# A 64-byte read of every ninth row of the modulation weights ahead of the loads of a DiT block

## The chip, the cores and the metric

The kernel runs on one core of a Trainium2 chip. The metric is device time in microseconds (us) of one execution; the median of several executions is compared. The profiled execution is one such execution, recorded by the hardware profiler; its span runs from the first to the last instruction of the program.

## The reference, cut to what matters

The reference is one DiT block (a diffusion transformer layer) on B, N, D = 2, 256, 1152, with 2 heads of 576 and an MLP of 4608; all inputs are bf16. The six modulation vectors come from the small input `c` through the weights `w_mod`.

```python
mod = (_silu(c) @ w_mod).reshape(B, 6, 1, D)
shift_a, scale_a, gate_a, shift_m, scale_m, gate_m = [mod[:, i] for i in range(6)]
h = _layernorm(x, axis=-1) * (1 + scale_a) + shift_a
qkv = (h @ wqkv).reshape(B, N, 3, H, Dh)
...
attn = _softmax(jnp.einsum('bqhd,bkhd->bhqk', q, k) * Dh ** (-0.5), axis=-1)
a = jnp.einsum('bhqk,bkhd->bqhd', attn, v).reshape(B, N, D) @ wo
x = x + gate_a * a
h2 = _layernorm(x, axis=-1) * (1 + scale_m) + shift_m
m = _gelu(h2 @ w_fc1) @ w_fc2
return x + gate_m * m
```

`w_mod` is a matrix of 1152 rows and 6912 columns. A row has 13,824 bytes, the whole 15.9 MB. Columns D to 2D hold `scale_a`.

## The kernel before, in words

The 512 tokens lie in four tiles of 128 partitions. All weights are streamed from HBM once, through one ordered list of loads on SyncE's queue (`dma`, L665, with `eng="sp"`): `x` in two loads (`ld_x0`, `ld_x1`), the scale columns of `w_mod` (`ld_sc0_*`: three loads, the first 640 columns of `scale_a`, in runs of 1280 bytes), the K weights row block by row block (`ld_wk*`), the rest of the scale columns (`ld_sc5_*`, runs of 1024 bytes of the same rows), and then the shift columns, Q, V, the other modulation columns, the output projection and the MLP weights. Only one load goes elsewhere: `c` (18 pieces of 256 bytes, `ld_c`, L692) is issued on ScalarE's queue.

The kernel builds a list of units with dependencies, and a planner (`Sched.schedule`, L281) puts them in order by a simple model of durations and landing times. TensorE (PE) and SyncE keep the order in which the program writes them. The first steps of VectorE (DVE) and ScalarE (ACT) are a list by hand (`S.first`, L909 to L915); the rest follows the planner. Every unit then waits on semaphores for what it depends on. A unit that writes a region of SBUF waits for the earlier writers of that region.

The start of the program, which the prediction follows step by step, is this:

- GpSimd (POOL) makes the identity matrix (L708 to L711); PE does two filler matmuls `warm_a` of 512 columns (L716 to L718).
- PE transposes `c` (`c_T`, L721), ScalarE takes its tanh (`c_tanh`, L722), VectorE turns it into SiLU (`c_half`, `c_silu`, L723 and L724). On PE 15 more filler matmuls `warm_b` (L773, called in L820) follow.
- VectorE (tiles 1 and 2) and ScalarE (tiles 0 and 3) take the LayerNorm statistics of `x` (`ln_stats_dve` L728, `ln_stats_act` L737), GpSimd the power -0.5, and VectorE writes the normalised rows (`xn_1`, `xn_0`, L753).
- PE transposes them (`xn_T`, L760), and between them multiplies the scale columns with SiLU(c), 128x2 at a time (`mod_kt`, L775), with single fillers between these (`warm_c`, `warm_d`, `warm_e`).
- VectorE adds 1 (`sc1a`, L783), then VectorE and ScalarE scale the transposed rows (`hk`, L786 to L792), and PE starts the K projection (`k_pair`, L804).

After that come Q, the scores and softmax, V, the transposes of the probabilities (`pt_transposes`, L953, whose copies write the tiles `PTS` at the offset `O_PT`), attention, output projection with the second LayerNorm, and the two MLP products.

All matmuls go through the helper at L686 and all transposes through L689, so these two lines stand for all of PE's work in the profile; all DMAs have L667.

Of the kernel before, what the change touches and what calls it, by code (L numbers as in the profile page):

```python
# [497 lines left out]
P = 128  # L498
NTOK = 512
D = 1152  # L500
KT = 9
# [40 lines left out]
def build_kernel(nc, x, c, wqkv, wo, w_mod, w_fc1, w_fc2, out):  # L542
# [5 lines left out]
    with (  # L548
# [4 lines left out]
        def sb(off, nbytes, dt=BF16):  # L553
            assert off % 4 == 0 and off + nbytes <= ARENA_BYTES, (off, nbytes)
            v = arena[:, off // 2:(off + nbytes) // 2]
            if dt == F32:
                v = v.bitcast(F32)
            return v
# [18 lines left out]
        O_PT = O_P + 4096  # L577
# [87 lines left out]
        def dma(dst, src, nbytes, name, is_out=False, eng="sp", run=4096):  # L665
            eff = 1.0 if run >= 4096 else (1.08 if run >= 2304 else (1.15 if run >= 1536 else (1.3 if run >= 1024 else 1.42)))
            return S.op(eng, 500.0 if eng == "sp" else 150.0, lambda e: e.dma_start(dst, src), reads=[src], writes=[dst],  # L667
                        name=name, dma_bytes=nbytes * eff, is_out=is_out)
# [20 lines left out]
            S.instr(lambda e: e.transpose(o, i_, idn), reads=[i_, idn], writes=[o])  # L689


        dma(CSB[0:18, :], c.rearrange("b (k p) -> (b k) p", p=P), 18 * 256, "ld_c", eng="act")  # L692
        for b in range(2):
            dma(X[:, 2 * b:2 * b + 2, :], xv[b], 2 * P * D * 2, "ld_x%d" % b)
# [200 lines left out]
        for kt in range(KT):  # L895
            for b in range(2):
# [5 lines left out]
                else:  # L902
# [7 lines left out]
            "dve": ["zq4b", "c_half", "c_silu", "bn_ln1_1_0", "bn_ln1_1_1", "bn_ln1_1_2", "aggr_ln1_1", "veps_ln1_1", "bn_ln1_2_0", "nvar_ln1_0", "veps_ln1_0",  # L910
                    "xn_1", "xn_0", "bn_ln1_2_1", "bn_ln1_2_2", "aggr_ln1_2", "veps_ln1_2", "nvar_ln1_3", "veps_ln1_3",
                    "sc1a_0", "hk_0_0", "xn_2", "hk_1_0", "xn_3", "hk_3_0", "hk_0_1", "hk_1_1", "hk_3_1", "hk_4_1", "sc1a_5"],
            "act": ["ld_c", "c_tanh", "sq_ln1_0", "sum_ln1_0", "sq_ln1_3", "sum_ln1_3", "xnT_cp0_8", "xnT_cp0_5", "hk_2_0", "hk_4_0",
                    "hk_2_1", "xnT_cp1_8", "xnT_cp1_5"],
        }  # L915

# [285 lines left out]
def bass_standalone__dit_block__diffusion_kernel(  # L1202
    nc: bass.Bass,
    x: bass.AP,
    c: bass.AP,
    wqkv: bass.AP,
    wo: bass.AP,
    w_mod: bass.AP,
    w_fc1: bass.AP,
    w_fc2: bass.AP,  # L1210
    out: bass.AP,
):
    build_kernel(nc, x, c, wqkv, wo, w_mod, w_fc1, w_fc2, out)
# [28 lines left out]
```

## Time and profile before

| what | value |
|---|---|
| median of 3 runs | 246.3 us (246.1 to 247.2) |
| profiled execution | 246.26 us |
| its span | 244.2 us |
| PE busy | 239.3 us, 98% of the span |
| weight loads on PE (PEld) | 146.8 us, 60% |
| VectorE busy | 98.7 us, 40% |
| ScalarE busy | 63.0 us, 26% |
| GpSimd busy | 21.5 us, 9% |
| read from HBM | 50.14 MB |

Times in the profile count from the start of the span. In the timeline a line begins with the start and the duration, then come engine, line, operation and form; a number after `x` is how many instructions are merged, and square brackets give the idle time ahead of it and what ended it. A name with a q (ACTq, SPq) is the queue of an engine's sequencer: there a DMA is issued, while the data move later. In the list of DMA issues the last number is the median time from issue to landing. In the chain of work that ended last a line has start, duration, engine and line.

### The profile page before, as it was taken

The page shows a single profiled execution, that of the slowest core. Times are in us where ns is not written, and L with a number is a line of the kernel's source. Part 1 is how long each engine was busy: PE and PEld are TensorE (multiplying, and loading weights), DVE is VectorE, ACT ScalarE, POOL GpSimd, SP SyncE. Part 2 cuts the span into 40 slices and gives each one's busy share as a digit, 9 for nine tenths or more (in the row PEclk, how much of TensorE's full clock was granted, in tenths as well). Part 3 has the DMA queues.
Part 4 walks back from the last instruction along what each step waited for, and adds up shares of the span by engine and source line. Part 5 has one row for each costly group of instructions (what it writes and reads, how often), then busy time and mean ns, then how long its engine had stood idle before and what let it go on. Part 6 is the DMA issues. An engine that isn't in the chain of part 4 may idle for free.

```text
span 244.2 us, 3973 instructions
## 1 busy us (share of the span) xinstructions
PE 239.3 (98%) x1721; PEld 146.8 (60%) x1731; DVE 98.7 (40%) x205; ACT 63.0 (26%) x128; POOL 21.5 (9%) x37
## 2 busy tenths in 40 slices
PE   7999999999999999999999999999999999999995
PEld 2689844466557666798544444444565656566575
DVE  3742450446323689879999600000022222111112
ACT  5730340235312306983322333222000000000000
POOL 1400000000021275600000110000000000000000
DMA  6999999999994999979943589200000000000000
GB/s 244 350 377 393 389 381 401 419 422 406 387 329 111 341 386 391 392 246 396 349 132 101 172 256 393 79 0 3 0 16 16 19 17 16 19 16 16 29 22 16
DMA packets 28875, 51.57 MB, mean 211 GB/s; under 512 B 1587, under 2 KB 15675, under 8 KB 28859
## 3 DMA queue, kind: packets, MB, share of 16 engines
q1 hardware_dynamic: 28384, 50.14, 56.9%
q0 software_dynamic: 448, 1.19, 2.0%
q8 instruction: 13, 0.21, 0.4%
q14 instruction: 3, 0.02, 0.0%
q10 hardware_dynamic: 27, 0.00, 0.0%
HBM read 50.14 MB, written 1.19 MB: 210 GB/s over the span
## 4 chain that ended last, share of the span: by engine, by line
PE 97%; ACT 1%; issue 0%; DVE 0%; POOL 0%; POOLq 0%
PE psum L686 95%; PE psum L689 2%; ACT arena L1091 1%; ACT arena L1073 1%; DVE arena L792 0%; POOL arena L709 0%; DVE arena L1184 0%; DVE arena L1185 0%; POOL arena L708 0%; DVE arena L783 0%; POOL arena L713 0%; POOLq L1227 0%
## 5 line engine op out<-in xcount | busy, mean ns | idle before, releaser
L686 PE MATMUL psum<-arena 128*128 128x384 bf16 (+9 forms) x1632 | 236.1, 312 | 2.2 <-POOL arena L709 1.4
L686 PEld LDWEIGHTS psum<-arena 128*128 128x128 bf16 (+1 forms) x1642 | 141.4, 97 | 92.3 <-issue 5.0
L1184 DVE TENSOR_TENSOR arena<-psum,arena 128x384 f32<-128x384 f32 (+3 forms) x14 | 7.0, 501 | 89.4 <-PE psum L686 89.4
L1101 ACT ACTIVATE arena<-psum 128x512 bf16<-128x512 f32 (+1 forms) x44 | 22.5, 522 | 42.6 <-PE psum L686 42.6
L681 ACT ACTIVATE arena<-psum 128x512 bf16<-128x512 f32 (+6 forms) x28 | 14.8, 549 | 40.1 <-PE psum L686 38.2
L683 DVE CAST arena<-psum 128x512 bf16<-128x512 f32 (+2 forms) x21 | 13.0, 627 | 26.5 <-PE psum L686 26.3
L1002 DVE SCALAR_TENSOR_TENSOR arena<-arena 128x1152 f32<-128x1152 bf16 x16 | 21.3, 1409 | 0.0
L1068 POOL TENSOR_TENSOR arena<-arena 128x384 f32<-128x384 f32 x12 | 11.0, 914 | 12.9 <-DVE arena L1067 11.7
L667 POOL DMA_DIRECT2D dit_scratch<-arena x4 | 2.6, 662 | 94.0 <-ACT arena L681 58.7
L731 DVE BATCH_NORM_STATS2 arena<-arena 128x6 f32<-128x384 f32 (+1 forms) x18 | 9.5, 549 | 1.2 <-DMA arena<-in_x_dram 1.1
L1073 ACT ACTIVATE arena<-arena 128x1152 bf16<-128x1152 f32 x4 | 5.4, 1353 | 9.5 <-DVE arena L1072 9.5
L1067 DVE TENSOR_TENSOR arena<-psum,arena 128x384 f32<-128x384 f32 x12 | 6.6, 548 | 3.2 <-PE psum L686 3.0
L689 PEld LDWEIGHTS psum<-arena 128*128 128x128 bf16 (+1 forms) x89 | 6.0, 98 | 2.4 <-DMA arena<-in_c_dram 0.8
L689 PE MATMUL psum<-arena 128*128 128x128 bf16 (+1 forms) x89 | 7.3, 219 | 0.1
L1185 DVE TENSOR_TENSOR arena<-arena 128x384 bf16<-128x384 f32 (+3 forms) x14 | 7.0, 501 | 0.5
L1091 ACT ACTIVATE arena<-psum,arena 128x128 bf16<-128x128 bf16 x16 | 6.1, 460 | 3.2 <-PE psum L689 2.5
L1088 DVE TENSOR_SCALAR arena<-psum,arena 128x128 bf16<-128x128 bf16 x20 | 5.5, 336 | 2.0 <-PE psum L689 1.8
L943 DVE TENSOR_REDUCE arena<-psum 128x2 f32<-128x512 f32 x4 | 2.8, 692 | 4.0 <-PE psum L686 3.7
L947 ACT ACTIVATE arena<-psum,arena 128x256 bf16<-128x256 f32 x8 | 3.7, 470 | 2.4 <-DVE arena L944 1.9
L735 POOL TENSOR_TENSOR arena<-arena 128x1 f32<-128x1 f32 x6 | 3.3, 555 | 6.1 <-DVE arena L734 6.1
L792 DVE TENSOR_SCALAR arena<-psum,arena 128x256 bf16<-128x256 bf16 x7 | 2.4, 348 | 3.6 <-PE psum L689 2.3
L900 ACT ACTIVATE arena<-arena 128x256 bf16<-128x256 bf16 x6 | 2.5, 495 | 3.3 <-DVE arena L894 3.3
(46 smaller groups left out, 43.1 us busy)
## 6 DMA issues: line engine op xcount, KB each, us to landing
arena<-in_w_mod_dram SPq DMA_DIRECT2D x4, 2592.0 KB, 20.2
arena<-in_w_fc_dram SPq DMA_DIRECT2D x9, 1152.0 KB, 8.2
arena<-in_w_fc_dram SPq DMA_DIRECT2D x4, 2592.0 KB, 17.4
arena<-in_wqkv_dram SPq DMA_DIRECT2D x18, 288.0 KB, 10.2
arena<-in_w_mod_dram SPq DMA_DIRECT2D x3, 864.0 KB, 13.2
arena<-in_wqkv_dram SPq DMA_DIRECT2D x1, 2592.0 KB, 10.9
arena<-in_wo_dram SPq DMA_DIRECT2D x1, 2592.0 KB, 32.7
arena<-in_w_mod_dram SPq DMA_DIRECT2D x3, 480.0 KB, 6.8
```

Source lines behind the costliest of these rows:

```text
L681: act(c_act(n), lambda e: e.activation(out=dst, in_=src, func=ACTF.Copy), [src], [dst], name)
L683: dve(c_dve_psum16(n) if psum16 else c_dve_psum32(n), lambda e: e.tensor_copy(dst, src), [src], [dst], name)
L686: S.instr(lambda e: e.matmul(o, lhsT=l, rhs=r, start=st, stop=sp, **kw), reads=[l, r], writes=[o])
L689: S.instr(lambda e: e.transpose(o, i_, idn), reads=[i_, idn], writes=[o])
L731: dve(550, lambda e, s=s, o=o: e.bn_stats(out=o, in_=s), [s], [o], "bn_%s_%d" % (tag, ci))
L1002: u = dve(1300, lambda e, o=o, w=w, s1=s1: e.scalar_tensor_tensor(out=o, in0=w, scalar=s1, in1=o, op0=ALU.mult, op1=ALU.add), [w, s1, o], ...
L1068: S.op("pool", 930, lambda e, xs=xs, x1c=x1c: e.tensor_tensor(out=x1c, in0=x1c, in1=xs, op=ALU.add), reads=[x1c, xs], writes=[x1c], name=" ...
L1073: act(1344, lambda e: e.activation(out=xn2, in_=x1, func=ACTF.Identity, scale=rs, bias=nm), [x1, rs, nm], [xn2], "xn2_%d" % t)
L1091: act(440, lambda e, o=o, dst=dst, s1=s1, s2=s2: e.activation(out=dst, in_=o, func=ACTF.Identity, scale=s1, bias=s2), [o, s1, s2], [dst], ...
L1101: act(c_act(ntok), lambda e: e.activation(out=dst, in_=o, func=ACTF.Gelu_apprx_tanh), [o], [dst], "gelu_%d_%d" % (f, tok0))
L1184: dve(c_dve_psum32(w), lambda e, o=o, gm=gm, t1=t1: e.tensor_tensor(out=t1, in0=o, in1=gm, op=ALU.mult), [o, gm], [t1], "fc2_t1_%d_%d" % ( ...
L1185: dve(c_dve_32(w), lambda e, t1=t1, x1c=x1c, ost=ost: e.tensor_tensor(out=ost, in0=t1, in1=x1c, op=ALU.add), [t1, x1c], [ost], "fc2_out_%d ...
```

## The change

One DMA is added ahead of `ld_c` on ScalarE's queue. It views `w_mod` as 128 groups of 9 rows and reads from the first row of each group 32 elements (64 bytes) at column D, where `scale_a` begins: 128 pieces, one for each partition, 8 KB in all. They land in the first 64 bytes of the tile `PTS[0]` on all partitions. Nothing reads them; the tile is overwritten with transposed probabilities later. The new unit `touch` stands first in ScalarE's list by hand.

```diff
+        dma(sb(O_PT, 64), w_mod.rearrange("(p k) f -> p k f", k=KT)[:, 0, D:D + 32], P * 64, "touch", eng="act")
         dma(CSB[0:18, :], c.rearrange("b (k p) -> (b k) p", p=P), 18 * 256, "ld_c", eng="act")
...
-            "act": ["ld_c", "c_tanh", "sq_ln1_0", "sum_ln1_0", "sq_ln1_3", "sum_ln1_3", "xnT_cp0_8", "xnT_cp0_5", "hk_2_0", "hk_4_0",
+            "act": ["touch", "ld_c", "c_tanh", "sq_ln1_0", "sum_ln1_0", "sq_ln1_3", "sum_ln1_3", "xnT_cp0_8", "xnT_cp0_5", "hk_2_0", "hk_4_0",
```

## The prediction

> **What bounds the kernel now.** I read the page first, then the chain of work that ended last in order of time, then the timeline of the first 12 us engine by engine, because the change sits in the first instruction of the program. The page's chain line:
>
> ```profile
> PE 97%; ACT 1%; issue 0%; DVE 0%; POOL 0%; POOLq 0%
> ```
>
> TensorE (PE) carries 97% of the span: after the start it runs matmul behind matmul to the end. The waits of PE and of its weight loader (PEld) on DMAs come to 0.8 us (for c) and 0.2 us (for w_mod), both in the first 11 us; on the big weights, nothing. So no later transfer is worth anything here, and whatever the start loses or gains goes through to the end. The start, by the chain:
>
> ```profile
> 1.42 1.03 PE psum L686 x2
> 2.45 0.12 PE psum L689
> 2.57 5.71 PE psum L686 x15
> 8.28 0.50 PE psum L689 x9
> ...
> 11.28 0.18 DVE arena L783
> 11.46 0.02 issue
> 11.48 0.36 DVE arena L792
> 11.85 0.05 issue
> 11.89 1.92 PE psum L686 x16
> ```
>
> Two filler matmuls, the transpose of c (2.45), fifteen more fillers until 8.28, the transposes of normalised x, the scale columns, then `sc1a` and the first `hk` on VectorE, and at 11.89 the first K matmul. There is no gap on PE from the transpose of c to 11.2: it is a fixed list in a fixed order, so it shifts as a whole when c is late. The weight loader shows what each step waited for:
>
> ```profile
> 2.38 0.10 PEld L689 LDWEIGHTS psum<-arena 18*128 18x128 bf16 x1 [0.84 <-DMA arena<-in_c_dram]
> ...
> 6.75 0.15 PEld L686 LDWEIGHTS psum<-arena 128*128 128x128 bf16 x1 [0.28 <-issue]
> 7.17 0.15 PEld L686 LDWEIGHTS psum<-arena 128*128 128x128 bf16 x1 [0.28 <-issue]
> 7.47 0.31 PEld L686 LDWEIGHTS psum<-arena 128*128 128x128 bf16 x2 [0.15 <-issue]
> 8.01 0.60 PEld L689 LDWEIGHTS psum<-arena 128*128 128x128 bf16 x9 [0.22 <-DVE arena L753]
> ...
> 10.46 0.81 PEld L686 LDWEIGHTS psum<-arena 128*128 128x128 bf16 x18 [0.23 <-DMA arena<-in_w_mod_dram]
> ```
>
> The transpose of c begins the moment c lands. The fillers start 0.427 us apart until 7.17 and 0.216 us apart from 7.47 on (starts of the single matmuls in the trace), so PE's clock doubles near 7.34. The stage table's PEclk column says 1.00 throughout and does not record this; the spacing does. The last line: the third piece of the scale weights is there at 10.46, 0.11 us ahead of the matmul that uses it (10.57).
>
> **The change, part by part.**
>
> *One more DMA issue on ScalarE, ahead of c.* ScalarE now and VectorE's first work:
>
> ```profile
> 0.78 0.60 ACTq L667 DMA_DIRECT2D arena<-in_c_dram  x1
> 1.42 1.28 ACT L722 ACT_TABLE_LOAD   x1 [1.42 <-PEq L1227]
> 2.71 0.19 ACT L722 ACTIVATE arena<-psum 128x18 f32<-128x18 bf16 x1
> 4.48 1.16 ACT L739 ACTIVATE arena<-arena 128x1152 bf16<-128x1152 bf16 x1 [1.58 <-DMA arena<-in_x_dram]
> ```
>
> An issue takes 0.60 us there; SyncE's take 0.37 to 0.55 for 128 to 384 pieces, so the touch's 128 pieces cost between 0.37 and 0.60. I take ScalarE's own 0.60. It pushes back the issue of c (to about 1.38), the table load behind it (to 2.02 to 3.30) and `c_tanh`. The table load stays hidden: `c_tanh` must wait for c anyway.
>
> *c now meets a busy queue.* In this trace c's 18 packets start at 1.76 to 1.86, x's first at 1.79: c gets through in front. Issued 0.60 later, each of its packets finds x packets (4608 bytes, 178 ns each in the packet records) ahead of it. Lower bound: nothing extra. Upper bound, from the DMA answer:
>
> ```profile
> dit_scratch<-arena POOLq DMA_DIRECT2D x2, 2.2 KB, 4.2
> dit_scratch<-arena POOLq DMA_DIRECT2D x1, 4.0 KB, 1.7
> ```
>
> Small transfers: 4.2 us beside the full load queue (70 us), 1.7 on an empty one (139 us); the difference is 2.5 us. Each DMA engine has two c packets, and I let each wait for one x packet: 2 x 0.178 = 0.36 us, nearer to the lower end because x has only just begun. So c is late by 0.60 + 0.36 = 0.96 us, bounds 0.4 to 3.1. The Trainium skill ("DMA: Bandwidth & Descriptors", Queues, rings and completion order) has each DMA engine take its queues in turn packet by packet; the packet records at 72.3 to 72.9, small packets between 1024-byte ones, agree, and by it alone the 0.36 would stand.
>
> *What lateness of c costs PE.* The fillers after the transpose begin at 2.50. Up to the clock change at 7.34 they fit 4.84/0.427 = 11.3 slow ones, the other 3.7 take 0.79: end 8.13, against 8.12 in the trace. With c late by d, d/0.427 fewer fit the slow stretch and that many more run at 0.216: the end moves by 0.216/0.427 = 0.506 d. For d = 0.96: **+0.49 us**, if the clock changes when it did.
>
> *What is late next.* VectorE, in its fixed order, does `c_half` and `c_silu` (end 3.40) ahead of the statistics of x (start 4.48): slack 1.08, and 0.96 fits. ScalarE's `c_tanh` ends 2.90 against 4.48: fits. `xn_1` ends at 7.95 against the transpose at 8.12, slack 0.17, which grows to 0.66 when PE comes 0.49 later. The scale weights' 0.11 grows to 0.60. So only PE's shift counts.
>
> *The touch's own packets.* 128 of 64 bytes, 8 on each of 16 engines, ahead of and among x's. Bounds: below, 8 packets at c's 15 ns, 0.12 us; above, 8 that each pay what the slowest first x packet paid over its usual, 8 x (706 - 178) ns = 4.2 us. I take the price of the slow first packets of w_mod (next part), 0.33, plus 0.12: x lands 0.45 later, inside the 0.66. Its target is the tile of the transposed probabilities, whose first writer (`pt_transposes`, about 59 us) gains a wait that is fulfilled tens of us before; nothing queues behind it. POOL's first DMA is at 70 us and is not passed.
>
> *What the touch may give.* The first pass over w_mod (1152 packets of 1280 bytes, 5 to 10 us) has 58 packets over 63 ns where the median is 55; their excess is 5.3 us over 16 engines, 0.33 us per engine. The second pass over the same rows (1024 bytes, 13 to 17 us) has none above 130 ns. So first contact does cost something, and the touch could take up to 0.33 us off the scale weights' landing. I cost this at nothing: the work that hides it is the filler list, which PE reaches that piece after (10.57, now 11.06). Uncovered, it would be worth 0.33 at most. Later w_mod loads land ahead of PE.
>
> *Order elsewhere.* PE and SyncE run in a fixed order, the others' start too. In the planner's model PE at this place waits for the normalised x, not c, so I expect no other step to change places: 0.
>
> Sum: +0.49 on the profiled execution's 246.26 us (span 244.2, 2.06 around it), which equals the median 246.3: **246.8 us**. About 0.5% (1.2 us) is what a measurement of this kernel can tell from no change, so this counts as within.
>
> **Rivals.**
> - *The clock comes later (slower).* PE now stands still between its first two fillers and c, 0.1 us; with the touch about 1.1 us. For: the slow stretch lasted 1.42 to 7.34, 5.92 us of work, and if a pause starts that count anew from the transpose at 3.34 it ends at 9.26, 1.92 us later; PE at half speed loses 0.96 of that. With 0.49: +1.45, **247.7**. It decides as soon as the pause is long enough to count as idle. Against: today's small pause did no visible harm, and nothing in one trace shows where the count began. The Trainium skill ("TensorE: Matmul & The Clock Gate", The HAM clock gate) says one fully busy, free-running window of 3.4 us opens the clock, so a pause matters only in some phases; here the doubled spacing agrees, the window cannot be seen. By it the change would come a whole window late or not at all: about +2.2 or +0.5.
> - *c and x stuck (slower).* With c late by 3.1, `c_silu` ends at 6.5 and holds up the statistics of x by 2.0: `xn_1` 9.97, PE +2.0, **248.3**. For: the 4.2 us row. Against: c's packets showed no such delay beside x's.
> - *c unharmed, x and weights earlier (faster).* PE can win only down to `xn_1`, 8.12 to 7.98: -0.14, **246.1**. For: first contact is slow in the trace. Against: c is issued second by construction.
> - *The touch does not do what it says*: the slow packets stay. The time is the forecast's, since nothing waits for them.
>
> **How the numbers follow.** Forecast 0.55; later clock 0.20; stuck 0.10; earlier 0.08; a gain over 0.5% by something that the trace does not show 0.07. Slower by over 0.5% (above 247.5): 0.10 and most of 0.20, so 0.27. Faster: 0.07. Within: 0.66. The range goes from the -0.14 less the runs' 0.15 scatter below the median (246.0) to the stuck case and its like, 248.4.
>
> **What would show it.** After the change: the c issue at about 1.4 on ScalarE's queue; the transpose of c at about 3.3; fillers 0.43 apart until about 7.3; transposes of x at 8.6; first K matmul at 12.4; from there the same distances to the end. Spacing of 0.43 beyond 8.5 speaks for the late clock; statistics of x well after 4.9 for the stuck case; a changed order of steps after 12 us, or a first K matmul before 11.9, would make the prediction wrong.

## The result, and the profile after

The changed kernel takes 248.52 us (median of 7, 247.78 to 249.64), the kernel before 246.79 us (median of 7: the three executions of the table above and four more): a ratio of 1.0082, 95% interval 1.0066 to 1.0098. By the ratio it is slower by about 2.0 us; the two medians differ by 1.73. The forecast was 246.8 us, and the measured time lies just above the end of its range, 248.4. The profiled execution took 248.51 us with a span of 246.5, 2.25 us more than the one before.

The chain of work that ended last, after the change (start, duration, what):

```profile
0.80 0.41 ACTq L667
1.21 0.03 issue
1.24 3.64 DMA arena<-in_c_dram
4.89 0.05 issue
4.93 0.19 PE psum L689
5.12 5.57 PE psum L686 x15
10.69 0.50 PE psum L689 x9
...
13.68 0.18 DVE arena L784
...
14.29 1.92 PE psum L686 x16
```

The chain now leads through the touch's issue on ScalarE and the load of `c`, a DMA that took no part in it before. The transpose of `c` begins at 4.93 instead of 2.38 us, the first K matmul at 14.29 instead of 11.89. From there to the last matmul it is 229.81 us, before 229.90: all of the loss is in the first 14 us. The weight loader, in the timeline:

```profile
4.93 0.10 PEld L689 LDWEIGHTS psum<-arena 18*128 18x128 bf16 x1 [3.38 <-DMA arena<-in_c_dram]
...
8.87 0.15 PEld L686 LDWEIGHTS psum<-arena 128*128 128x128 bf16 x1 [0.28 <-issue]
9.30 0.15 PEld L686 LDWEIGHTS psum<-arena 128*128 128x128 bf16 x1 [0.28 <-issue]
9.66 0.53 PEld L686 LDWEIGHTS psum<-arena 128*128 128x128 bf16 x3 [0.22 <-issue]
10.31 0.70 PEld L689 LDWEIGHTS psum<-arena 128*128 128x128 bf16 x9
```

Two things moved. `c` is late by 2.55 us. And the spacing of the fillers stays at 0.427 us until 9.30; interpolated as in the prediction, the clock changes at 9.60 instead of 7.34. The formula of the prediction, with both measured numbers, gives the whole shift: 2.55 x 0.506 = 1.29 from the lateness, and 2.26 x (1 - 0.506) = 1.12 from the later clock, together 2.41, where the first transpose of `x` moved from 8.12 to 10.53. ScalarE and VectorE, after:

```profile
0.80 0.41 ACTq L667 DMA_DIRECT2D arena<-in_w_mod_dram  x1
1.24 0.61 ACTq L667 DMA_DIRECT2D arena<-in_c_dram  x1
1.89 1.28 ACT L723 ACT_TABLE_LOAD   x1 [1.89 <-issue]
5.16 0.19 ACT L723 ACTIVATE arena<-psum 128x18 f32<-128x18 bf16 x1 [1.99 <-PE psum L689]
5.68 0.18 DVE L725 SCALAR_TENSOR_TENSOR arena<-arena 128x18 bf16<-128x18 f32 x1
5.77 1.47 DVE L732 BATCH_NORM_STATS2 arena<-arena 128x6 f32<-128x384 bf16 x3
8.39 0.58 DVE L754 TENSOR_SCALAR arena<-arena 128x1152 bf16<-128x1152 bf16 x1
```

The issue of `c` moved by only 0.46 us (0.78 to 1.24), yet it takes 3.69 us from there to the transpose instead of 1.60. The statistics of `x` (L732) now queue behind `c_silu` on VectorE and begin at 5.77 instead of 4.48; `xn_1` ends at 8.97, still 1.6 us ahead of PE.

### The profile page after: what moved, and what is told of

It is laid out like the page before. It is cut to its first block, busy times and chain, and to the rows that moved or that the text cites. A ratio compares the mean times of both kernels' runs of the same rounds, so it can differ in the third digit from the quotient of the medians.

```text
span 246.5 us, 3975 instructions
## 1 busy us (share of the span) xinstructions
PE 239.1 (97%) x1721; PEld 146.7 (60%) x1731; DVE 98.5 (40%) x205; ACT 62.9 (26%) x128; POOL 21.5 (9%) x37
## 4 chain that ended last, share of the span: by engine, by line
PE 95%; DMA 1%; ACT 1%; issue 0%; DVE 0%; ACTq 0%
PE psum L686 93%; PE psum L689 2%; DMA arena<-in_c_dram 1%; ACT arena L1092 1%; ACT arena L1074 1%; ACTq L667 0%; DVE arena L793 0%; DVE arena L1185 0%; DVE arena L1186 0%; DVE arena L784 0%
## 5 line engine op out<-in xcount | busy, mean ns | idle before, releaser
L732 DVE BATCH_NORM_STATS2 arena<-arena 128x6 f32<-128x384 f32 (+1 forms) x18 | 9.5, 548 | 0.1
```

Source lines behind the costliest of these rows:

```text
L732: dve(550, lambda e, s=s, o=o: e.bn_stats(out=o, in_=s), [s], [o], "bn_%s_%d" % (tag, ci))
```

## The experiments

Three theories at first. **A**: `c` is late because it stands behind the touch in the same queue, each touch packet taking its turn with a packet of `x`. **B**: the touch's reads themselves do harm, by scattered rows or by holding up the engines. **C**, formed after the first four runs: any small DMA issued behind the loads of `x` comes late, touch or not. On the price, the question was what the pause on TensorE does to the clock. Each experiment was profiled once; the lines below are from that execution, the ratios from all. In the code shown, `...` stands for what is not needed to see the edit.

**touch_second**, the touch issued behind `c`:

```diff
-        dma(sb(O_PT, 64), w_mod..., "touch", eng="act")
         dma(CSB[0:18, :], c..., "ld_c", eng="act")
+        dma(sb(O_PT, 64), w_mod..., "touch", eng="act")
```

> The touch is issued behind the load of c instead of ahead of it. Theory A (c is late because it stands behind the touch on ScalarE's queue): c is transposed at about 2.4 us again, the first K matmul is back at 11.9 to 12.0, and the time is that of the kernel before within 0.2%. Rival B (the touch's own reads disturb x and the weights, wherever they stand in the queue): the first K matmul stays over 1 us late and the time stays 0.5% or more above before.

The weight loader's line for `c`:

```profile
3.14 0.10 PEld L689 LDWEIGHTS psum<-arena 18*128 18x128 bf16 x1 [1.59 <-DMA arena<-in_c_dram]
```

Ratio to before 0.9998 (0.9982 to 1.0015). The touch behind `c` costs nothing that the times show, against B. The profile fits neither expectation: `c` was transposed at 3.14, not 2.4, and the first K matmul came at 12.67, 0.78 late. Two of the 18 packets of `c` began only at 2.73 and 2.74, though it was issued at 0.79, 0.01 us ahead of `x`. The two are in a race even here, and so without a touch: in c_behind_before, below, two packets of `c` began at 2.29 and 2.30.

**touch_near**, 128 neighbouring pieces of row 0:

```diff
-        dma(sb(O_PT, 64), w_mod.rearrange("(p k) f -> p k f", k=KT)[:, 0, D:D + 32], P * 64, "touch", eng="act")
+        dma(sb(O_PT, 64), w_mod[0:1, 0:P * 32].rearrange("o (p f) -> (o p) f", f=32), P * 64, "touch", eng="act")
```

> The touch reads 128 pieces of 64 bytes that lie side by side in row 0 of w_mod, instead of one in every ninth row: as many packets, no scattered rows. Theory A (packets that take turns with x): nothing changes, c is transposed at 4.7 to 5.1, time within 0.2% of the changed kernel. Rival B (the scattered rows make the touch's reads begin 0.8 us later, 2.64 us where x begins at 1.80): the touch's packets begin at about 1.8, and c is transposed at about 4.1 or before; time 0.6 us or more below the changed kernel.

The touch's packets begin at 2.44 us, `c` is transposed at 4.63 us; ratio 1.0051 (1.0034 to 1.0068). The late beginning stays without scattered rows, so B's reason falls. The time is lower than the changed kernel's by less than the two intervals allow to separate, more than A expected. In this profile the clock changed at 8.66, and the first K matmul came at 13.68.

**touch_16**, one packet for each engine instead of eight:

```diff
-        dma(sb(O_PT, 64), w_mod.rearrange("(p k) f -> p k f", k=KT)[:, 0, D:D + 32], P * 64, "touch", eng="act")
+        dma(sb(O_PT, 64)[0:16, :], w_mod.rearrange("(p k) f -> p k f", k=KT * 8)[:, 0, D:D + 32], 16 * 64, "touch", eng="act")
```

> The touch reads 16 pieces (every 72nd row) instead of 128: one packet on each of 16 engines instead of eight. Theory A (turns with x, about 0.18 us for each touch packet on an engine): seven turns fewer, 1.3 us, so c is transposed at about 3.6, or at 2.9 if the late beginning goes as well. Rival B (c is late because a scattered read goes first, however many): c is transposed at 4.5 or later.

Seven turns fewer and no clear gain: ratio 1.0073 (1.0054 to 1.0091). The weight loader's line for `c`:

```profile
4.83 0.10 PEld L689 LDWEIGHTS psum<-arena 18*128 18x128 bf16 x1 [3.29 <-DMA arena<-in_c_dram]
```

A expected 3.6 or less. In the packet records the touch's last packet begins at 3.14 and the first of `c` at 3.64, so turns taken with touch packets were not what held `c` up. A falls as well, and since scattered rows were already excluded, what remained was the moment at which `c` is issued: theory C. One thing speaks against reading C too simply: here and in touch_near the touch itself was issued 0.01 us ahead of the first load of `x` (0.79 against 0.80 here, 0.78 against 0.79 there), and its packets began 0.51 and 0.65 us behind those of `x`. A lead of 0.01 us was enough for `c` in the kernel before, and not for the touch.

**late_c**, no touch; `c` is issued after a small copy on ScalarE (the memset on GpSimd that fills what the copy reads moves up in the program text, to stand ahead of it):

```diff
+        act(300, lambda e: e.activation(out=CSB[0:18, :], in_=ONES[0:18, :], func=ACTF.Copy), [ONES], [CSB[0:18, :]], "delay")
         dma(CSB[0:18, :], c.rearrange("b (k p) -> (b k) p", p=P), 18 * 256, "ld_c", eng="act")
...
-            "act": ["ld_c", "c_tanh", "sq_ln1_0", ...
+            "act": ["delay", "ld_c", "c_tanh", "sq_ln1_0", ...
```

> No touch at all: the load of c waits for a small operation on ScalarE (a copy into the tile of c, which the load then overwrites), so that it is issued at about 2.4 us, well behind the loads of x, as first and only DMA of ScalarE's queue. Theory C (any small DMA that is issued behind the loads of x waits for the packets that the engines have already taken in): from the issue of c to its transpose 3.4 us or more, as behind the touch (3.4 to 3.7), so c is transposed at 5.8 or later, the first K matmul comes at 14.5 or later, and the time is 0.9% or more above before, without any touch. Rival A (c is late because the touch stands ahead of it in the same queue): from issue to transpose 1.6 to 2.2 us, c transposed at 4.0 to 4.6, time 0.5 to 0.7% above before.

From the timeline:

```profile
2.43 0.59 ACTq L667 DMA_DIRECT2D arena<-in_c_dram  x1
...
7.56 0.10 PEld L689 LDWEIGHTS psum<-arena 18*128 18x128 bf16 x1 [6.01 <-DMA arena<-in_c_dram]
```

5.13 us from issue to transpose, with nothing else on ScalarE's queue, the first K matmul at 16.44, and a ratio of 1.0199 (1.0174 to 1.0223). The touch is not needed to make `c` late.

**c_delay_short** and **c_delay_long**, no touch; the issue of `c` waits for one memset of 0.1 us on VectorE, ahead of or behind VectorE's first one (the load overwrites what the memset wrote):

```diff
+        dve(100, lambda e: e.memset(CSB[0:18, :], 0.0), [], [CSB[0:18, :]], "delay")
         dma(CSB[0:18, :], c.rearrange("b (k p) -> (b k) p", p=P), 18 * 256, "ld_c", eng="act")
...
-            "dve": ["zq4b", "c_half",
+            "dve": ["delay", "zq4b", "c_half",    (short)
+            "dve": ["zq4b", "delay", "c_half",    (long)
```

> No touch. The issue of c waits for a small memset of its tile, first on VectorE (0.91 to about 1.0 us), so it goes out at about 1.1 us instead of 0.78, and everything else stays. Theory C (what counts is only that the issue of c comes behind that of x, by however little): from issue to transpose 3.3 us or more, c transposed at 4.4 or later, time 0.5 to 0.9% above before. Rival A (the touch ahead of c in the same queue is what makes c late): c transposed at 2.7 to 3.1, time within 0.3% of before.

> The same with the memset behind VectorE's first one, so that c is issued at about 1.3 us, near the 1.24 us that it has behind the touch. Theory C: from issue to transpose about 3.6 us as in the changed kernel, c transposed at 4.7 to 5.2, time 0.6 to 1.0% above before, as the changed kernel. Rival A: c transposed at 2.9 to 3.3, time within 0.4% of before.

Short, then long:

```profile
1.01 0.59 ACTq L667 DMA_DIRECT2D arena<-in_c_dram  x1
...
4.42 0.10 PEld L689 LDWEIGHTS psum<-arena 18*128 18x128 bf16 x1 [2.88 <-DMA arena<-in_c_dram]
```

```profile
1.28 0.58 ACTq L667 DMA_DIRECT2D arena<-in_c_dram  x1
...
4.53 0.10 PEld L689 LDWEIGHTS psum<-arena 18*128 18x128 bf16 x1 [2.98 <-DMA arena<-in_c_dram]
```

Ratios 1.0063 (1.0046 to 1.0081) and 1.0060 (1.0046 to 1.0073). The short one, set against the kernel before, is the cleanest comparison: an issue that is 0.23 us later, now behind the first load of `x` (0.80) and still ahead of the second (1.24), makes `c` 2.05 us later and the kernel 0.6% slower. The long one has `c` issued 0.04 us later than behind the touch and gives 2.15 of the changed kernel's 2.55 us; theory C had expected its transpose at 4.7 or later, and it came at 4.53. Its interval overlaps that of the changed kernel. In the packet records the first packet of `c` begins at nearly the same time in both, 3.70 and 3.67, and the last at 3.93 and 4.17; but in the short one, without a touch, the 18 packets are spread as widely (3.26 to 3.79). Whether the touch adds the other 0.4 itself is not settled.

**c_on_sync**, the touch first on ScalarE's queue, `c` on SyncE's queue ahead of `x`:

```diff
-        dma(CSB[0:18, :], c..., 18 * 256, "ld_c", eng="act")
+        dma(CSB[0:18, :], c..., 18 * 256, "ld_c")
...
-            "act": ["touch", "ld_c", "c_tanh",
+            "act": ["touch", "c_tanh",
```

> The touch stays first on ScalarE's queue, and c goes to SyncE's queue as its first load, ahead of x. Theory C: c is ahead of x again and is transposed at 2.4 to 3.2; x comes some 0.4 us later; the time is within 0.3% of before although the touch still runs. Rival B (the touch itself holds up the engines): c is transposed at 4 us or later and the time stays 0.6% or more above before.

```profile
0.79 0.38 ACTq L667 DMA_DIRECT2D arena<-in_w_mod_dram  x1
0.80 0.40 SPq L667 DMA_DIRECT2D arena<-in_c_dram  x1
1.26 0.83 SPq L667 DMA_DIRECT2D arena<-in_x_dram  x2
...
2.39 0.10 PEld L689 LDWEIGHTS psum<-arena 18*128 18x128 bf16 x1 [0.84 <-DMA arena<-in_c_dram]
...
8.36 0.51 PEld L689 LDWEIGHTS psum<-arena 128*128 128x128 bf16 x9 [0.52 <-DVE arena L754]
...
11.31 0.72 PEld L686 LDWEIGHTS psum<-arena 128*128 128x128 bf16 x18 [0.73 <-DMA arena<-in_w_mod_dram]
```

With the touch still running, `c` is back at 2.39. Ratio 1.0025 (1.0013 to 1.0037): the loads of `x` and the weights go out about 0.45 us later, and the weight loader's waits for `xn_1` and for the scale weights grow from 0.22 and 0.23 us to 0.52 and 0.73. The first K matmul comes at 12.62.

**fillers_first**, the touch ahead of `c`, six fillers moved ahead of the transpose of `c`:

```diff
-        for i in range(2):
+        for i in range(8):
             S.unit("pe", 430.0, "warm_a%d" % i)
...
-        warm(15, "b")
+        warm(9, "b")
```

> The touch stays ahead of c, but six of the fifteen fillers behind the transpose of c are put ahead of it, so TensorE has no pause while c is on its way. Theory A (about half of the 2.4 us is the clock, which changes 2.3 us later because of the pause): the spacing of the fillers halves at about 7.3 us, TensorE is through the fillers at about 8.1 and then waits for xn_1 (about 9.0), and the first K matmul comes at 12.8, 1.5 us earlier than with the touch; time about 0.9 us above before. Rival B (the lateness of c alone, 2.55 us, is the price, and the clock changes by itself): the clock changes at about 9.6 as with the touch, and the first K matmul comes at 13.9 or later.

```profile
5.11 0.10 PEld L689 LDWEIGHTS psum<-arena 18*128 18x128 bf16 x1 [1.00 <-DMA arena<-in_c_dram]
...
9.20 0.51 PEld L689 LDWEIGHTS psum<-arena 128*128 128x128 bf16 x9 [2.04 <-DVE arena L754]
```

The same number of matmuls, `c` as late as before the move (5.11), and the ratio falls to 1.0029 (1.0014 to 1.0044). The clock changed at 5.9, earlier than the expected 7.3; then TensorE waited for `xn_1`, as expected, which `c_silu` holds up. The first K matmul came at 12.99 instead of 14.29. The ratio hides two groups: eight executions took 246.97 to 247.17 us at a mean granted clock of 0.999 to 1.0, the profiled one among them, and four took 248.12 to 248.31 us at 0.993. No trace of the four was kept. That the clock fell back in the wait for `xn_1`, which now comes behind the fillers, is possible and not shown.

**c_behind_before** and **c_behind_touch**, `c` off the path, without and with the touch:

```diff
-        (the transpose of c with c_tanh, c_half, c_silu, c_silu32, ahead of the statistics)
...
-        warm(15, "b")
+        warm(8, "b")
+        (the same lines)
+        warm(7, "b2")
...
-            "dve": ["zq4b", "c_half", "c_silu", "bn_ln1_1_0", ... "xn_1", "xn_0",
+            "dve": ["zq4b", "bn_ln1_1_0", ... "xn_1", "c_half", "c_silu", "xn_0",
-            "act": [..., "ld_c", "c_tanh", "sq_ln1_0", "sum_ln1_0",
+            "act": [..., "ld_c", "sq_ln1_0", "sum_ln1_0", "c_tanh",
```

> The kernel before, with c taken off the path: the transpose of c stands behind ten of the seventeen fillers, its tanh behind the two sums of ScalarE, c_half and c_silu behind xn_1 on VectorE. Theory C with the clock (the count of the clock starts when TensorE works without a pause, here at 1.4 us instead of 2.5): the fillers end at 7.0 to 8.6, xn_1 at about 8.0 becomes the bound, the first K matmul comes at 11.7 to 12.3; time equal to before or up to 0.3% below. Rival (the pause does not matter): equal to before.

> The changed kernel with c taken off the path in the same way. Theory C (all of the loss is c's lateness on the path; the touch costs and gives nothing else): the time equals that of the same kernel without the touch within 0.2%, 0.6 to 1.0% below the changed kernel. Rival B (the touch itself disturbs the loads): 0.4% or more above the same kernel without the touch. Rival D (the touch makes the weights come earlier): 0.2% or more below it.

Ratios 1.0003 (0.9991 to 1.0014) and 0.9999 (0.9986 to 1.0011). The weight loader, without the touch and with it:

```profile
5.79 0.10 PEld L689 LDWEIGHTS psum<-arena 18*128 18x128 bf16 x1 [0.84 <-issue]
...
8.01 0.50 PEld L689 LDWEIGHTS psum<-arena 128*128 128x128 bf16 x9 [0.52 <-DVE arena L746]
```

```profile
5.79 0.10 PEld L689 LDWEIGHTS psum<-arena 18*128 18x128 bf16 x1 [0.84 <-DMA arena<-in_c_dram]
...
8.13 0.51 PEld L689 LDWEIGHTS psum<-arena 128*128 128x128 bf16 x9 [0.52 <-DVE arena L747]
```

When TensorE does not wait for `c`, the touch costs and gives nothing that the times show: the loss came from `c`'s lateness on the path. (In these two profiles the first K matmul came at 11.80 and 12.20, the scale weights being later with the touch; the times of eleven executions of each do not show it.) Neither version is clear of the kernel before: with the fillers out of the way, `xn_1` bounds the start at 8.0.

In the changed kernel and the ten experiments, the time of the profiled execution less the start of its first K matmul lies between 233.9 and 234.3 us (before: 246.26 - 11.89 = 234.4). To within half a microsecond the start decides everything. And the start itself adds up: in the seven profiles where the fillers wait behind a late `c` (after, touch_second, touch_near, touch_16, late_c and the two delays), 0.506 times the lateness of `c` plus 0.494 times that of the clock change gives the shift of the first K matmul within 0.01 us. touch_near and touch_16 show how much the clock alone can do: `c` was transposed 0.20 us apart, the clock changed at 8.66 and 10.28, and the first K matmuls came 0.90 us apart.

## Why the prediction was wrong

- *What bounds the kernel*: right. PE's list shifts as a whole, and the chain shows it.
- *One more issue on ScalarE, 0.60 us*: 0.41 measured, and the issue of `c` 0.46 later, inside the bounds.
- *"I let each wait for one x packet: 2 x 0.178 = 0.36 us, nearer to the lower end because x has only just begun"*: this is the step that failed first. `c` was late by 2.55 us, 0.46 from the later issue and 2.09, not 0.36, from the longer way from issue to transpose. The row used for the upper bound (a small transfer beside the full queue, 2.5 us more) was the nearer one: in all runs where `c` has no lead over `x` and TensorE waits for it, 3.2 to 3.9 us passed from issue to transpose, and 5.1 when issued at 2.43. The first packet of `c` begins 2.2 to 2.6 us after its issue in these runs, and 3.8 in late_c, instead of 1.0. By then 98 to 128 of the 128 packets of the first load of `x` had begun, so six to eight on each of the 16 DMA engines; in late_c all 256 of `x` and 267 of `w_mod`. `c` does not wait for one packet of `x` for each of its own. It comes behind most of a load. The turns as such are there (while the touch's 128 packets begin, from 2.64 to 4.17, 110 packets of `x` begin). But the 0.36 does not follow from the rule that the prediction names beside them: in the Trainium skill ("DMA: Bandwidth & Descriptors", Queues, rings and completion order) an engine drains a whole packet of one queue before the next, and typically a packet holds some 9 to 17 descriptors (a descriptor is the order for one move of bytes), while the prediction counted one packet of the profile's records for each turn. Whether such groups, the writing of descriptors or packets already taken in hold `c` up, no run here shows.
- *"The end moves by 0.506 d, if the clock changes when it did"*: the second step that failed. It changed 2.26 us later, as the rival of the late clock had it, and brought 1.12 us. The Trainium skill ("TensorE: Matmul & The Clock Gate", The HAM clock gate) asks for one busy window of about 3.4 us at a free phase, so, as an estimate from that figure, 3.4 to 6.8 us of work. The runs agree: counted from the first filler behind one of the longer pauses (0.7 to 5.1 us), the change comes after 3.6 (late_c), 3.9, 4.3, 4.4, 4.5, 4.9 and 5.3 us. Where the pause for `c` was 0.3 us or less, it comes 4.5 to 6.0 us after the very first filler (fillers_first 4.5, the two c_behind 5.3 and 5.6, before 5.9, c_on_sync 6.0), in fillers_first and the two c_behind within 1.1 us behind that pause. So it is the long pause that starts the count anew. How long the count then lasts differs by 1.8 us from profile to profile, and with one profile of each kernel the split of the 2.41 us into 1.29 and 1.12 holds for these two executions only. In the seven profiles between 80% and 110% of the lateness of `c` reaches the first K matmul, not half.
- *What is late next*: the slack of 1.08 us on VectorE was right, and 2.55 went past it; `xn_1` came 1.02 late. With the fillers' end at 10.53 instead of 8.12 this stayed hidden. In fillers_first it is what TensorE waits for.
- *The touch's own packets, x 0.45 late*: 0.01 and 0.18 us for the two halves of `x`. Too high, and of no consequence.
- *What the touch may give*: nothing came. The first pass over `w_mod` again has 58 packets over 63 ns, with 0.38 us of excess per engine (0.33 before; 0.30 to 0.49 in the other runs without a touch). So the touch does not remove them, and that they come from first contact, as the prediction took it, is not shown. (The second pass, which the prediction compares, runs to 18.7 us, not 17.) Its rival that the touch doesn't do what it says holds, and c_behind_touch confirms that nothing was gained in time either.
- *The rivals*: the late clock (247.7) and the stuck `c` (248.3) were priced singly, as alternatives. They are one event: what makes `c` late makes the pause, and the pause makes the clock late. The prediction's formula with both measured sizes gives 246.26 + 2.41 = 248.7, and the profiled execution took 248.5. Each rival was right in one half. The stuck `c` had the lateness nearly right (3.1 against 2.55 us) but the path wrong: its time goes by way of a late `xn_1`, which held up nothing here, so that 248.3 lies so near is luck. The late clock had the path right, but took the whole 5.92 us of the slow stretch as the count (measured from the transpose: 4.67) and `c` late by 0.96 only; the two errors largely cancel in its 1.92 us, so that its nearness to 2.26 is luck as well.

## What to carry to other kernels

Issue a small load that the first steps wait for clearly ahead of the bulk loads of every queue, not only of its own: here a few tenths of a microsecond decided between 1.6 us and 3.2 to 5.1 us. Where filler work brings TensorE's clock up, a long wait in front of the fillers is paid twice, as delay and as a later clock. Putting fillers ahead of what may be late, or letting that thing be used later, took most or all of the loss away here, though the first of these left a wait behind the fillers, and four of twelve executions took about 1.1 us longer than the other eight. And rivals with a common cause are not alternatives: price them together.

## What the runs showed of the hardware that was not expected

The time from the issue of a small DMA to the use of its data does not grow smoothly with the moment of its issue: 1.60 us to the transpose when issued at 0.78, together with `x`; 3.42 at 1.01; 3.25 at 1.28; 5.13 at 2.43. Even together with `x` it can lose some of the race (2.35 us in touch_second, issued at 0.79). When the first packets of `c` begin late, most of the 128 packets of the first load of `x` have begun (98 to 128). The profile's PEclk shows full speed where the spacing of the matmuls shows half, in the first 6 to 11 us of each profile.
